# Attention into a gated feed-forward: the first three token chunks take the f-tiles in three groups

## The chip, the cores and the metric

One core of a Trainium2 chip runs the whole program. The metric is the device time of one execution in microseconds. The engines are named as in the profile: PE (TensorE, matmuls), DVE (VectorE), ACT (ScalarE), POOL (GpSimd) and SP (the queue that issues the plain transfers).

## What is computed

Eight batches of eight-head attention (576 positions, head size 64) feed a gated feed-forward over all 8 x 576 = 4608 tokens. Four heads see a window of 32 positions, four see every 32nd position, so most of the score matrix is never formed.

```python
scores = (q @ k.T) / sqrt(64)                     # heads 0-3: 0 <= i-j < 32; heads 4-7: i >= j and i%32 == j%32
attn = exp(scores - max); attn = attn / (attn.sum(-1) + 1e-9)
x = (attn @ v) -> [4608, 512]                     # heads side by side
h = x @ w_in                                      # [4608, 2048]
sp = maximum(h, 0) + log1p(exp(-abs(h)))
out = (h * erf(sp)) @ w_out                       # [4608, 512]
```

## The kernel before

**Tiles.** The tokens form 12 chunks of 384; the 2048 hidden columns form 16 f-tiles of 128. One `ftile` is one chunk by one f-tile, so there are 192, in the order chunk by chunk, f = 0 to 15 inside. A first product (`mm1`, L585, 12 matmuls: `w_in` and x each as a high and a low part, the low-by-low term left out) fills a PSUM bank `h`; a chain of five DVE and six ACT operations makes the gated value and splits it into `ghi` and `glo` (n1 to n7, gate, prod, split_hi, split_lo, L590 to L626); a second product (`mm2`, L656, three matmuls for each of three token tiles t) adds `ghi` and `glo` times `w_out` into the PSUM banks `o0`, `o1`, `o2`. After f-tile 15 of a chunk ACT copies each `o` bank to an SBUF buffer `ob` (L671) and SP stores it. There are three `h` banks, one bank for each of the three `o`, and one buffer `ps` of two banks.

**Weights.** The weights arrive as 64-bit words. Each of the 32 groups of 128 x 512 (16 of `w_in`, 16 of `w_out`) takes four DVE operations and one ACT operation: `bits0` (L536), `bits1` and `bits2` (L543, L549), the ACT copy of the high part (L554), and `split_lo_w` (L557). They pass through a staging buffer of the tag `ob`, of which there are three, shared with the `ob` of the stores. The f-tiles 4s to 4s+3 need the four `w_in` groups of s; f-tile f needs the `w_out` group f.

**Attention.** `heads` handles a pair of heads of one batch, so there are 32 pairs. A pair is: scores on PE (L320, for the first two batches with the mask added by PE, L333), maximum and difference on DVE, exponent on ACT, sum and reciprocal on DVE, normalisation on POOL (`norm`, L418), transposes on PE (L427), a copy on ACT, the product with v on PE (L446), and a split of x into `xhi` and `xlo`. Chunks 0 to 2 need batches 0 and 1 (chunk 0 batch 0 alone), and so on by twos. For batch 0 the scores and the transposes lie in `h` or `o` banks (`B0`), three of its pairs lie in weight buffers not yet filled (`HOME`), and each pair's exponent adds up its row sums on ACT (L392, one operation for each 64 columns). Batch 1 uses the buffer `ps` alone for scores, transposes and output.

**Order.** `Plan` puts all operations on five engine queues when the program is built: each operation has a key (a due time from the tables of constants), and a list schedule with estimated durations takes the one with the lowest key among those that can start soonest. The result is a fixed order for each engine; on the chip an engine waits at whatever instruction is next in its order. Until the first `mm1`, PE's free time is filled with dummy matmuls (`warm`, L751).

Of the kernel before, what the change touches and what calls it, by code (L numbers as in the profile page):

```python
# [8 lines left out]
F32 = mybir.dt.float32  # L9
# [19 lines left out]
PRO = 74.154117  # L29
SLOT = 8.3314687  # L30
MM2 = 14.137159
W1K = (7.7180495, 48.67362, -5.03539, 67.675242)
W1S = (6.27419, 17.806925, 11.8133, 26.168915)
W2K = 61.550152
W2S = 10.390137
A0K = -5.727881
A0S = 1.5429374
A0D = 20.718269
A1K = 99.646963
A1S = -4.8860706  # L40
A1D = -7.3440005
QE = (15.200212, 8.5225749)
QO = (-5.0071746, 2.7270014)
QD = (0.4017474, 1.2188811, 1.98055, 1.78394, 1.3902936)
B0 = (("h", "h"), ("o0", "o1"), ("h", "h"), ("o0", "o1"))
HOME = (None, (7, 8, 9), (10, 11, 12), (13, 14, 15))
ASH = 2.7979051
ADT = 2.5612463
BACKLOG = 1.1130116

# [35 lines left out]

def sub_block(t, j):

    if t == 4:
        return 16 + j % 2  # L90
    return 4 * (t // 2) + j + 8 * (t % 2)
# [10 lines left out]
class Op:  # L102
    def __init__(self, eng, dur, key, emit, after, new, use, earliest):
        self.eng, self.dur, self.key, self.emit, self.earliest = eng, dur, key, emit, earliest
        self.after, self.new = list(after), list(new)
        self.start = self.end = None
        self.locks = eng == "pool" or eng == "dve" and emit.__name__ in TWO
        for b in self.new + list(use):
            b.users.append(self)


class Plan:
# [8 lines left out]
    WINDOW = 70  # L121
# [25 lines left out]
    def order(self):  # L147
# [4 lines left out]
        while left:  # L152
# [24 lines left out]
            if e == "sp":  # L177
                free[e] = t + 0.6
                dma = max(dma, t + 0.6) + o.dur
                o.end = dma + 2.0  # L180
            else:
                o.end = free[e] = t + o.dur
                if o.locks:
                    held[e] = o.end
# [7 lines left out]
def attention_moe(  # L192
# [25 lines left out]
    con = cpool.tile([P, NCON], BF16, name="con")  # L218
    mask_l = con[:, :320]
# [27 lines left out]
    def heads(b, hp, key, dt, ring, before=(), pe_mask=False, pool_norm=True, act_sum=False, banks=None, home=None):  # L247
# [5 lines left out]
        if home is None:  # L253
            qk = [buf("apool", "qk", [P, WQ], f"qk_{pid}")]
            v = [buf("apool", "v", [P, WV], f"v_{pid}")]
        else:
            qk = [buf("wpool", f"w{NFC + f}", [P, 2 * SW], f"qk{f}_{pid}") for f in home[:2]]
            v = [buf("wpool", f"w{NFC + home[2]}", [P, 2 * SW], f"v_{pid}")] + qk[1:]
        sm = buf("apool", "sm", [P, 2, 384], f"sm_{pid}")
        pt = buf("apool", "pt", [P, 2, 384], f"pt_{pid}")  # L260
# [10 lines left out]
        t = s if banks else region(None, "t")  # L271
# [14 lines left out]
        def keys(rows, k0):  # L286
# [24 lines left out]
        def scores():  # L311
# [5 lines left out]
            for t, j, h, m in todo:  # L317
# [5 lines left out]
                    keys(rows, q0),  # L323
# [113 lines left out]
        def av():  # L437
# [5 lines left out]
            for m, a, h in todo:  # L443
# [3 lines left out]
                    px[h * D : (h + 1) * D, m, a * n : (a + 1) * n],  # L447
# [5 lines left out]
        def views(m, x):  # L453
            base = (b % 2) * S
            if loc:
                n = 320 if m else 256
                return px[:, m, :n], x[:, base + 256 * m : base + 256 * m + n]
            nr = 14 if m else 18
            dst = x[:, base : base + S].rearrange("p (a r) -> p a r", r=32)[:, :, 18 * m : 18 * m + nr]
            return px[:, m, : 18 * nr].rearrange("p (r a) -> p a r", a=NA), dst  # L460
# [14 lines left out]
        lq = add("sp", P * 4 * (WL if loc else WS) / 3.6e5, key - 8.0, load_qk, new=qk)  # L475
        lv = add("sp", P * 4 * (VL if loc else VS) / 3.6e5, key - 7.0, load_v, [lq], v[:1], v[1:])
        d_s = 0.85 if loc else 0.95
        if pe_mask:
            d_s += 2 * cols / 2400.0 + 0.05
        o_s = add("pe", d_s, key, scores, [lq, *o_con, *before], [*s, sm], qk)  # L480
        o_n, first = [], []
        for i, p in enumerate(parts):
# [3 lines left out]
            if not pe_mask:  # L486
                o = add("dve", dve(n), key + QD[0] * dt + e, mask(i), [o], [], [z])
            o = add("dve", dve(n), key + QD[0] * dt + 0.05 + e, maxi(i), [o] + first[:1], [mx] if i == 0 else [], [z, mx])
            first.append(o)
            if act_sum:  # L490
                o = add("dve", 0.12, key + QD[0] * dt + 0.1 + e, negate(i), [o], [], [mx])
                o = add("act", 0.33 * n / 64, key + QD[1] * dt + 0.1 + e, exp_sum(i), [o] + first[1:2], [rc] if i == 0 else [], [z, mx, sm, rc])
            else:
                o = add("dve", dve(n), key + QD[0] * dt + 0.1 + e, less(i), [o], [], [z, mx, sm])
                o = add("act", act(n), key + QD[1] * dt + 0.1 + e, exp(i), [o], [], [sm])
                o = add("dve", dve(n), key + QD[2] * dt + e, total(i), [o] + first[1:2], [rc] if i == 0 else [], [sm, rc])
            first.append(o)
            o = add("dve", 0.25, key + QD[2] * dt + 0.05 + e, invert(i), [o], [], [rc])
            if pool_norm:
                o = add("pool", 0.1 + n / 450.0, key + QD[2] * dt + 0.1 + e, norm(i), [o], [], [sm, rc])  # L500
            else:
                o = add("dve", dve(n), key + QD[2] * dt + 0.1 + e, norm(i), [o], [], [sm, rc])
            y = t[i] if len(t) > 1 else t[0]
            o = add("pe", 0.33 * (p.stop - p.start), key + QD[3] * dt + e, turn(i), [o] + first[2:3], ([pt] if i == 0 else []) + ([y] if not banks else []), [sm, y])
            first.append(o)
            o = add("act", act(384 * (p.stop - p.start), 0.06), key + QD[3] * dt + 0.1 + e, fetch(i), [o], [], [y, pt])
            o_n.append(o)
        o_v = add("pe", 1.3 if loc else 0.95, key + QD[4] * dt, av, o_n + [lv] + ring, [px], [pt, *v])
        done = []
        for m in range(2):  # L510
            n = (320 if m else 256) if loc else (252 if m else 324)
            hi, lo = split(m)
            o = add("act", act(n, 0.06), key + QD[4] * dt + 0.1 + 0.01 * m, hi, [o_v], [], [px])
            done.append(add("dve", dve(n), key + QD[4] * dt + 0.2 + 0.01 * m, lo, [o], [], [px]))
        return done, o_v


    def weight(i, src, rows, sl, key):
# [41 lines left out]
        if wide:  # L560
            op = add("sp", P * 8 * n / 3.6e5, key - 8.0, load, new=[words])
            op = add("dve", dve(n, 0.5), key, bits0, [op], [w], [words])
            op = add("dve", dve(n), key + 0.1, bits1, [op], [], [w, words])
            op = add("dve", dve(n), key + 0.2, bits2, [op], [], [w, words])
        else:
            op = add("sp", P * 4 * n / 3.6e5, key - 8.0, load, new=[w])
        op = add("act", act(n), key + 0.3, split_hi, [op], [pair], [w])
# [3 lines left out]
    def ftile(k, ready):  # L571

        c, f = k // NFC, k % NFC
# [57 lines left out]
        def at(offset):  # L631
            return v0 + (offset + 0.3) * SLOT / 3.9

        first = add("pe", 2.09, v0, mm1, ready[0] + mm1_first[-1:], [ph])
        o = add("act", tp, at(0.0), n1, [first], [a], [ph])
        o = add("dve", td, at(0.6), n2, [o], [], [ph, a])
        o = add("act", ta, at(1.2), n3, [o], [], [a])
        o = add("act", ta, at(2.25), n4, [o], [bb], [a])
        o = add("dve", td, at(2.9), n5, [o], [], [a, ph])
        o = add("dve", td, at(3.5), n6, [o], [], [a, bb])  # L640
        o = add("act", ta, at(4.35), n7, [o], [], [bb])
        o = add("act", ta, at(5.55), gate, [o], [], [bb])
        o = add("dve", td, at(6.2), prod, [o], [], [bb, ph])
        o_h = add("act", tp, at(6.8), split_hi, [o] + hi_of[-1:], [ghi], [ph])
        hi_of.append(o_h)
        o_l = add("dve", td, at(7.9), split_lo, [o_h], [glo], [ph, ghi])
        last = []
        for t in range(NTT):
            if f == 0:
                o_ps[t] = buf("ps_o", f"o{t}", [P, DM], f"o{t}_{c}")  # L650
# [197 lines left out]
```

## Time and profile before

| | |
|---|---|
| median of 3 runs (lowest to highest) | 960.15 us (959.93 to 961.97) |
| the profiled execution's own time | 961.45 us |
| its span, first to last instruction | 959.7 us |
| busy: PE, DVE, ACT, POOL | 933.7, 689.4, 652.0, 47.5 us |
| mean granted TensorE clock | 0.987 |
| DMA packets | 64.23 MB, of which 9.44 MB written |

The numbers of busy time are sums over the whole span. PE counts the dummy matmuls as busy, so a busy PE in the first tenth says little. The first 120 us differ from the rest in what they wait for, and are read by windows.

### The profile page before, as it was taken

Reading aid. Unit: us, or ns where it says so; the run is one execution under the profiler, and the core shown is the slowest. Engines: PE = TensorE matmul, PEld = TensorE weight load, DVE = VectorE, ACT = ScalarE, POOL = GpSimd, SP = SyncE. Lnnn points to the kernel's source line nnn. Section 1 sums busy time; section 2 is a strip of 40 time slices with the busy share of each in tenths; the row PEclk is TensorE's granted clock in tenths of the full one; section 3 lists DMA queues with packets and bytes.
Section 4 is the critical chain, followed back from the end, with each engine's and each line's share of the span. In section 5 each row is a group of like instructions: output and inputs, shape, how many; then the busy total and the mean of one; then the engine's idle time right before and its main releaser. Section 6 shows DMA issues by size and latency. Waiting matters only on the chain.

```text
span 959.7 us, 20411 instructions
## 1 busy us (share of the span) xinstructions
PE 933.7 (97%) x8380; PEld 832.5 (87%) x8380; DVE 689.4 (72%) x1350; ACT 652.0 (68%) x1437; POOL 47.5 (5%) x40
## 2 busy tenths in 40 slices
PE   8948999999999999999999999999999999999998
PEld 6837788998888899988888889988888899999997
DVE  4999999766776666676878566666777666666664
ACT  5555778676667766766667766766667766666765
POOL 1111000000101000000001000000000000000000
PEclk9978999999999999999999999999999999999999
DMA  9963101003111210002312210001220200000000
GB/s 354 395 245 129 54 1 60 28 26 109 67 53 62 66 48 1 34 27 62 112 54 70 79 32 22 34 27 45 101 81 2 95 1 1 34 1 1 34 1 33
DMA packets 19822, 64.23 MB, mean 67 GB/s; under 512 B 2192, under 2 KB 2320, under 8 KB 19728
## 3 DMA queue, kind: packets, MB, share of 16 engines
q1 hardware_dynamic: 19728, 62.92, 18.5%
q8 instruction: 66, 1.08, 0.4%
q14 instruction: 28, 0.23, 0.1%
HBM read 53.48 MB, written 9.44 MB: 66 GB/s over the span
## 4 chain that ended last, share of the span: by engine, by line
PE 89%; DVE 8%; issue 1%; ACT 1%; DMA 1%; SPq 0%
PE o L656 41%; PE h L585 40%; PE x L446 3%; PE s L320 2%; PE t L427 2%; DVE w L543 2%; DVE w L549 1%; DVE pair L557 1%; DMA words<-w_in 1%; DVE w L536 1%; DVE a L590 1%; ACT sm L392 1%; DVE mx L356 0%; DVE xlo L470 0%; DVE b L590 0%
## 5 line engine op out<-in xcount | busy, mean ns | idle before, releaser
L656 PE MATMUL o<-pair,ghi 128*128 128x512 f32 x1152 | 365.4, 398 | 0.0
L585 PE MATMUL h<-xhi,pair 128*128 128x384 f32 x1536 | 303.3, 339 | 1.9 <-DVE glo L626 1.8
L585 PEld LDWEIGHTS h<-xhi,pair 128*128 128x128 f32 x1536 | 273.9, 189 | 13.4 <-DVE glo L626 3.1
L656 PEld LDWEIGHTS o<-pair,ghi 128*128 128x128 f32 x1152 | 210.8, 189 | 39.0
L593 ACT ACTIVATE b<-b 128x384 f32<-128x384 f32 x384 | 201.3, 524 | 58.4 <-DVE b L590 55.0
L656 PE MATMUL o<-pair,glo 128*128 128x512 f32 x576 | 226.8, 394 | 0.0
L590 DVE SCALAR_TENSOR_TENSOR a<-a,h 128x384 f32<-128x384 f32 x192 | 105.7, 550 | 87.1 <-ACT b L593 87.1
L585 PE MATMUL h<-xlo,pair 128*128 128x384 f32 x768 | 165.1, 336 | 0.0
L593 ACT ACTIVATE a<-a 128x384 f32<-128x384 f32 x192 | 100.8, 525 | 80.9 <-DVE a L590 80.9
L620 DVE TENSOR_TENSOR h<-b,h 128x384 f32<-128x384 f32 x192 | 107.1, 558 | 50.1 <-ACT b L593 50.1
L593 ACT ACTIVATE a<-h 128x384 f32<-128x384 f32 x192 | 93.1, 485 | 72.9 <-PE h L585 71.6
L626 DVE TENSOR_TENSOR glo<-h,ghi 128x384 fp32r<-128x384 f32 x192 | 106.2, 553 | 49.1 <-ACT ghi L623 48.2
L585 PEld LDWEIGHTS h<-xlo,pair 128*128 128x128 f32 x768 | 136.9, 189 | 0.0
L590 DVE SCALAR_TENSOR_TENSOR a<-h,a 128x384 f32<-128x384 f32 x192 | 106.4, 554 | 41.8 <-ACT a L593 41.6
L656 PEld LDWEIGHTS o<-pair,glo 128*128 128x128 f32 x576 | 108.4, 188 | 23.6
L623 ACT CAST ghi<-h 128x384 fp32r<-128x384 f32 x192 | 91.1, 474 | 39.0 <-PE o L656 29.5
L590 DVE SCALAR_TENSOR_TENSOR b<-b,a 128x384 f32<-128x384 f32 x192 | 110.9, 578 | 2.0
L593 ACT ACTIVATE b<-a 128x384 f32<-128x384 f32 x192 | 100.1, 522 | 3.2
L418 POOL TENSOR_TENSOR sm<-sm,r 128x768 f32<-128x768 f32 (+3 forms) x36 | 47.3, 1314 | 699.1 <-DVE r L411 546.1
L446 PEld LDWEIGHTS x<-pt,v 64*64 64x64 f32 x1848 | 32.9, 136 | 11.5 <-issue 3.6
L320 PEld LDWEIGHTS s<-qk 64*32 64x32 f32 (+1 forms) x1872 | 25.1, 121 | 17.2 <-issue 13.3
L446 PE MATMUL x<-pt,v 64*64 64x32 f32 (+1 forms) x1848 | 36.8, 223 | 1.9 <-ACT pt L433 1.8
(40 smaller groups left out, 508.1 us busy)
## 6 DMA issues: line engine op xcount, KB each, us to landing
v<-v_loc SPq DMA_DIRECT2D x15, 640.0 KB, 4.0
out<-ob SPq DMA_DIRECT2D x36, 256.0 KB, 2.2
qk<-qk_loc SPq DMA_DIRECT2D x15, 592.0 KB, 4.0
qk<-qk_str SPq DMA_DIRECT2D x14, 608.0 KB, 3.9
words<-w_in SPq DMA_DIRECT2D x16, 512.0 KB, 9.8
words<-w_out SPq DMA_DIRECT2D x16, 512.0 KB, 9.2
v<-v_str SPq DMA_DIRECT2D x16, 384.0 KB, 3.1
qk<-qk_str SPq DMA_DIRECT2D x4, 304.0 KB, 8.0
```

The costliest lines, as they stand in the source:

```text
L320: yield nc.tensor.matmul(bank(s, h)[m * j : m * (j + 1), 64 * t : 64 * (t + 1)], queries(rows, q0, m), keys(rows, q0), start=(h, j) not in ...
L418: yield (nc.gpsimd if pool_norm else nc.vector).tensor_tensor(out=d, in0=d, in1=spread(rc, i), op=ALU.mult)
L427: yield nc.tensor.transpose(bank(t, h)[:, 128 * w : 128 * w + 128], sm[:, h, c : c + 128], ident)
L446: yield nc.tensor.matmul(px[h * D : (h + 1) * D, m, a * n : (a + 1) * n], values(rows, (2 * a + h) * D), pt[rows, h, c : c + n], start=Tru ...
L543: yield nc.vector.scalar_tensor_tensor(out=wb, in0=words[:, :, 1], scalar=0xC0000000, in1=wb, op0=ALU.bitwise_and, op1=ALU.bitwise_or)
L585: yield nc.tensor.matmul(ph[:, :CH], win[4 * s + cc][:, w, fs], x[cc][:, c0 : c0 + CH], start=(i == 0), stop=(i == len(terms) - 1))
L590: yield nc.vector.scalar_tensor_tensor(out=out, in0=in0, scalar=scalar, in1=in1, op0=op0, op1=op1)
L593: yield nc.scalar.activation(dst, src, func, bias=bias[i], scale=scale)
L620: yield nc.vector.tensor_tensor(out=ph[:, :CH], in0=bb.tile, in1=ph[:, :CH], op=ALU.mult)
L623: yield nc.scalar.copy(ghi.tile, ph[:, :CH])
L626: yield nc.vector.tensor_tensor(out=glo.tile, in0=ph[:, :CH], in1=ghi.tile.bitcast(F32), op=ALU.subtract)
L656: yield nc.tensor.matmul(po.tile, g[:, ts], wout[f][:, w], start=(f == 0 and i == 0), stop=(f == NFC - 1 and i == 2),)
```

## The change

**The order of the f-tiles.** For chunks 0 to 2 the f-tiles are taken in three groups, 0 to 3, 4 to 7 and 8 to 15: all three chunks go through a group before the next group begins (`SEGS`). The 9 segments each end with the three `o` banks being copied to `ob`. The first segment of a chunk stores its partial sum as before; the two later ones add theirs to the output in memory by a transfer that POOL issues (`accumulate`), each waiting for the landing of the earlier transfer to the same rows. That makes 18 accumulating transfers of 256 KB and 18 more ACT copies. Chunks 3 to 11 go as before.

**The pairs ahead of them.** All eight pairs of batches 0 and 1 now use one set of banks for scores, transposes and output (`own=True`), among `h`, `o` and `ps` (`PAIRS`). Seven lie in weight buffers, three of them with a fourth buffer for the exponents; the transposed values overwrite the queries (`View`). The normalisation of pair 0_0 goes to DVE. The row sums on ACT are used by 0_0, 0_1, 0_3, 1_1 and 1_3. Loads of the weight groups that share a buffer with a pair are ordered behind it (`w_load`).

**The rest.** An exponent of one column is put ahead so that ACT loads its table early (`first_exp`). All keys are new tables (`FT` for the steps of an f-tile, `KW` for weights, `KP` for pairs), `WINDOW` is 250.

```diff
-PRO = 74.154117
-SLOT = 8.3314687
+PRO = 28
+SLOT = 4.5
+FT = (2.47591, 2.44924, 3.30228, ...
+PAIRS = (
+    (("h", "h"), None, True, False),
+    (("o0", "o1"), (4, 5, 6), True, True),
+    (None, (7, 20, 21, 22), False, True),
+    (("h", "h"), (23, 8, 9, 10), True, True),
+    (("o0", "o1"), (11, 24, 25, 26), False, True),
+    (None, (27, 12, 13), True, True),
+    (("o0", "o1"), (14, 15, 28), False, True),
+    (None, (29, 30, 31), True, True),
+)
+SEGS = ((0, 0, 4), (1, 0, 4), (2, 0, 4), (0, 4, 8), (1, 4, 8), (2, 4, 8), (0, 8, 16), (1, 8, 16), (2, 8, 16))
...
-        px = buf("ps_a", "ps", [P, 2, 512], f"x_{pid}")
...
-        t = s if banks else region(None, "t")
+        t = s if own else region(None, "t")
+        px = s if own else region(None, "x")
...
-            if f == NFC - 1:
+            if f == last_f:
...
+                def accumulate(t=t, ob=ob):
+                    yield nc.gpsimd.dma_start(
+                        out=out[c * CH + t * P : c * CH + (t + 1) * P, :], in_=ob.tile, accum_op=ALU.add
+                    )
...
-                add("sp", P * DM * 4 / 3.6e5, o.key + 0.1, store, [o], [], [ob])
+                if first_f == 0:
+                    stored[c, t] = add("sp", P * DM * 4 / 3.6e5, o.key + 0.1, store, [o], [], [ob])
+                else:
+                    o = add("pool", 1.2, o.key + 0.1, accumulate, [o, stored[c, t]], [], [ob])
+                    o.tail = 2.5
+                    stored[c, t] = o
...
-        for c in range(3 * p2, 3 * p2 + 3):
-            chunk(c)
+        for c, f0, f1 in SEGS if p2 == 0 else [(c, 0, NFC) for c in range(3 * p2, 3 * p2 + 3)]:
+            chunk(c, f0, f1)
```

**Where it shows in the order: DVE among the early f-tiles.** This is DVE's order before, between the gated value of f-tile 4 and `glo` of f-tile 5. In the names, `w` is the staging buffer of a weight group with its number, `pair` its finished form, and `a`, `b`, `h`, `glo` are the buffers of f-tiles.

```order
L536 TENSOR_SCALAR w_22_1592<-words_918 128x512
L590 SCALAR_TENSOR_TENSOR b_1581<-b_1581,a_1491 128x384
L557 TENSOR_TENSOR pair_1587<-w_14_1449,pair_1587 128x512
L543 SCALAR_TENSOR_TENSOR w_22_1592<-words_918,w_22_1592 128x512
L626 TENSOR_TENSOR glo_1607<-h_1392,ghi_1584 128x384
L549 SCALAR_TENSOR_TENSOR w_22_1592<-words_918,w_22_1592 128x512
L590 SCALAR_TENSOR_TENSOR a_1594<-h_1562,a_1594 128x384
L620 TENSOR_TENSOR h_1429<-b_1581,h_1429 128x384
L557 TENSOR_TENSOR pair_1624<-w_22_1592,pair_1624 128x512
L536 TENSOR_SCALAR w_23_1633<-words_954 128x512
L626 TENSOR_TENSOR glo_1638<-h_1429,ghi_1629 128x384
```

And this is DVE's order after the change, between the f-tiles 6 and 8 (counted in the new order).

```order
L589 TENSOR_SCALAR w_20_1526<-words_967 128x512
L644 SCALAR_TENSOR_TENSOR a_1510<-h_1477,a_1510 128x384
L596 SCALAR_TENSOR_TENSOR w_20_1526<-words_967,w_20_1526 128x512
L674 TENSOR_TENSOR h_1369<-b_1492,h_1369 128x384
L602 SCALAR_TENSOR_TENSOR w_20_1526<-words_967,w_20_1526 128x512
L644 SCALAR_TENSOR_TENSOR a_1510<-a_1510,h_1477 128x384
L644 SCALAR_TENSOR_TENSOR a_1541<-h_1512,a_1541 128x384
L644 SCALAR_TENSOR_TENSOR b_1534<-b_1534,a_1510 128x384
L610 TENSOR_TENSOR pair_1548<-w_20_1526,pair_1548 128x512
L680 TENSOR_TENSOR glo_1563<-h_1369,ghi_1555 128x384
```

Before, six of eleven rows are of weight groups; after, four of ten, because twelve f-tiles share the first eight groups.

**POOL's queue.** Before, POOL holds the normalisations of the pairs and nothing else; these are the last of the first two batches and the first of the next.

```order
L418 TENSOR_TENSOR sm_2_1004<-sm_2_1004,r_2_1068 128x768
L418 TENSOR_TENSOR sm_1_1114<-sm_1_1114,r_1_1214 128x2x320
L418 TENSOR_TENSOR sm_0_1264<-sm_0_1264,r_0_1345 128x2x320
L418 TENSOR_TENSOR sm_0_1517<-sm_0_1517,r_0_2204 128x2x320
L418 TENSOR_TENSOR sm_1_2160<-sm_1_2160,r_1_2306 128x2x320
```

After, the accumulating transfers (`out<-ob`) stand among them; the number behind `ob` is the f-tile whose segment it closes.

```order
L468 TENSOR_TENSOR sm_3_1082<-sm_3_1082,r_3_1165 128x768
L731 DMA out<-ob_15_2019 128x512
L731 DMA out<-ob_15_2028 128x512
L468 TENSOR_TENSOR sm_0_1425<-sm_0_1425,r_0_2046 128x2x320
L731 DMA out<-ob_15_2098 128x512
L731 DMA out<-ob_19_2212 128x512
L731 DMA out<-ob_19_2271 128x512
L731 DMA out<-ob_19_2274 128x512
L731 DMA out<-ob_23_2390 128x512
```

The first normalisation of batch 2 now stands behind two transfers, and 16 further transfers follow up to the end of the third chunk's last segment.

More of the change, by code (lines that the diff above doesn't have):

```diff
@@ L120 @@
     PATIENCE = 0.002
-    WINDOW = 70
+    WINDOW = 250
     def __init__(self, bufs):
@@ L181, in order @@
             else:
-                o.end = free[e] = t + o.dur
+                free[e] = t + o.dur
+                o.end = free[e] + o.tail
                 if o.locks:
-                    held[e] = o.end
+                    held[e] = free[e]
             for b in o.new:
@@ L244, in act, with heads @@
         return fixed + n / 1200.0
-    def heads(b, hp, key, dt, ring, before=(), pe_mask=False, pool_norm=True, act_sum=False, banks=None, home=None):
+    def heads(b, hp, keys, ring, before=(), pe_mask=False, pool_norm=True, act_sum=False, banks=None, home=None, own=False):
         loc = hp < 2
@@ L284, in queries, with keys_of @@
             return qk[0][rows, q0 : q0 + n]
-        def keys(rows, k0):
+        def keys_of(rows, k0):
             k0 += wq if home is None else 0
@@ L322, in scores @@
                     queries(rows, q0, m),
-                    keys(rows, q0),
+                    keys_of(rows, q0),
                     start=(h, j) not in used,
@@ L474, in heads @@
         add = plan.add
-        lq = add("sp", P * 4 * (WL if loc else WS) / 3.6e5, key - 8.0, load_qk, new=qk)
-        lv = add("sp", P * 4 * (VL if loc else VS) / 3.6e5, key - 7.0, load_v, [lq], v[:1], v[1:])
-        d_s = 0.85 if loc else 0.95
+        slab = pt if home is None else qk[0]
+        k_q, k_v, k_s, k_m, k_n, k_t, k_x = keys
+        lq = add("sp", P * 4 * (WL if loc else WS) / 3.6e5, k_q, load_qk, new=qk)
+        lv = add("sp", P * 4 * (VL if loc else VS) / 3.6e5, k_v, load_v, [lq], v[:1], v[1:])
+        d_s = 0.95 if loc else 1.0
         if pe_mask:
             d_s += 2 * cols / 2400.0 + 0.05
-        o_s = add("pe", d_s, key, scores, [lq, *o_con, *before], [*s, sm], qk)
+        o_s = add("pe", d_s, k_s, scores, [lq, *o_con, *before], [*s, sm], qk)
         o_n, first = [], []
@@ L503, in heads @@
             y = t[i] if len(t) > 1 else t[0]
-            o = add("pe", 0.33 * (p.stop - p.start), key + QD[3] * dt + e, turn(i), [o] + first[2:3], ([pt] if i == 0 else []) + ([y] if not banks else []), [sm, y])
+            o = add("pe", 0.33 * (p.stop - p.start) + 0.05, k_t + e, turn(i), [o] + first[2:3], ([pt] if i == 0 and home is None else []) + ([y] if not own else []), [sm, y])
             first.append(o)
-            o = add("act", act(384 * (p.stop - p.start), 0.06), key + QD[3] * dt + 0.1 + e, fetch(i), [o], [], [y, pt])
+            o = add("act", act(384 * (p.stop - p.start), 0.06), k_t + (0.1 + e), fetch(i), [o], [], [y, slab])
@@ L507, in heads @@
             o_n.append(o)
-        o_v = add("pe", 1.3 if loc else 0.95, key + QD[4] * dt, av, o_n + [lv] + ring, [px], [pt, *v])
+        o_v = add("pe", 1.35 if loc else 1.0, k_x, av, o_n + [lv] + ring, [] if own else px, [slab, *v] + (px if own else []))
         done = []
@@ L701, in attention_moe @@
             rows, sl = slice(c * P, (c + 1) * P), slice(f, f + SW)
-            op, pair = weight(i, w_in, rows, sl, W1K[i // 4] + W1S[i // 4] * (i % 4))
+            op, pair = weight(i, w_in, rows, sl, KW[i // 8][i % 8])
             w1.append(op)
@@ L706, in attention_moe, with chunk @@
         rows, sl = slice(f * P, (f + 1) * P), slice(0, DM)
-        op, pair = weight(NFC + f, w_out, rows, sl, W2K + W2S * f)
+        op, pair = weight(NFC + f, w_out, rows, sl, KW[2 + f // 8][f % 8])
         w2.append(op)
         wout.append(pair)
-    def chunk(c):
+    def chunk(c, f0, f1):
         need = [o for b in (2 * (c // 3), 2 * (c // 3) + 1) for o in x_of.get((b, c % 3), [])]
-        for f in range(NFC):
-            k = c * NFC + f
+        for f in range(f0, f1):
             ready = (need + w1[4 * (f // 4) : 4 * (f // 4) + 4], [w2[f]])
-            mm1_of[k], _ = ftile(k, ready)
-            mm1_first.append(mm1_of[k])
+            o, _ = ftile(len(mm1_first), c, f, f0, f1 - 1, ready)
+            mm1_first.append(o)
+            mm1_of[c] = o
     def chunks_of(b, hp, m):
```

173 lines of the change are left out of this document (104 added, 69 removed), and 4 rows, old and new, of the table KW.

## The prediction

> **What bounds the kernel now.** I read the page first, then windows, then PE's timeline and the chain of waits over the first 150 us.
>
> ```profile
> PE 933.7 (97%) x8380; PEld 832.5 (87%) x8380; DVE 689.4 (72%) x1350; ACT 652.0 (68%) x1437; POOL 47.5 (5%) x40
> DVE  4999999766776666676878566666777666666664
> PEclk9978999999999999999999999999999999999999
> ```
>
> Over the span PE is the bound and DVE is not. Slices 2 to 7 of DVE's row (each 24 us) say otherwise for the first stage, and PE's clock falls below full there alone. The windows have it in numbers; columns are length, then busy time and instructions of PE, PEld, DVE, ACT, POOL, granted clock, DMA share and GB/s.
>
> ```profile
> 0.00:24.00 24.00, 19.96 (x396) 16.26 (x397) 12.00 (x34) 13.21 (x70) 4.68 (x9) 1.00 0.94 354
> 24.00:48.00 24.00, 23.93 (x378) 21.17 (x377) 23.89 (x53) 13.59 (x47) 3.31 (x3) 1.00 1.00 395
> 48.00:72.00 24.00, 11.52 (x255) 9.60 (x254) 23.31 (x41) 12.83 (x25) 3.72 (x2) 0.71 0.66 245
> 72.00:96.00 24.00, 20.13 (x343) 17.84 (x342) 22.49 (x44) 12.90 (x27) 2.99 (x2) 0.87 0.39 129
> 96.00:120.00 24.00, 22.12 (x183) 19.09 (x182) 24.00 (x50) 16.91 (x38) 0.00 (x0) 0.99 0.17 54
> 120.00:144.00 24.00, 24.00 (x115) 21.46 (x114) 22.78 (x46) 17.59 (x37) 0.00 (x0) 0.94 0.00 1
> ```
>
> From 24 to 120 us DVE is busy 93.7 of 96 us. The transfers run at full share until 48 us and then fall off, so they feed DVE and don't bound it later. PE's timeline shows the two ends of that stage (start, length, what, idle before it).
>
> ```profile
> 45.14 1.66 PE L585 MATMUL h<-xhi,pair 128*128 128x384 f32 x8
> 55.61 0.93 PE L320 MATMUL s<-qk 64*64 64x64 f32 x48 [2.65 <-DVE sm L368]
> 118.32 2.11 PE L585 MATMUL h<-xhi,pair 128*128 128x384 f32 x8 [1.83 <-DVE glo L626]
> ```
>
> The first product of f-tile 0 starts at 45.14. The last wait of PE on DVE ends at 118.32, where f-tile 10 starts. Counted in the timeline between the two, PE begins ten first products and does 21 of the three-matmul groups of the second (seven f-tiles). From 118.32 to the end at 959.7 PE never waits: 841.4 us for 182 first products, 555 groups and 24 pairs. The chain shows PE's pace there, and DVE's pace ahead of it, where each instruction starts as the last one lets it (start, length, what).
>
> ```profile
> 24.69 0.34 DVE w L536
> ...
> 49.23 0.60 DVE pair L557
> 50.44 0.60 DVE w L543
> 51.04 0.47 DVE a L590
> ...
> 52.71 0.87 DVE mx L356
> ...
> 124.32 2.10 PE h L585 x12
> 126.42 2.08 PE o L656 x9
> ```
>
> So a first product takes 2.10 and a second 2.08, 0.69 for each group. On DVE a weight group takes 0.34 + 3 x 0.60 = 2.14 us and an f-tile 5 x 0.47 = 2.35. Before, an f-tile of chunk 0 needs a `w_out` group and, on average, a `w_in` group of its own: 2.35 + 4.28 = 6.6 us of DVE against 4.18 of PE. That is why PE idles.
>
> **The three groups.** The first 12 f-tiles after the change need 8 weight groups, and so do the next 12: (8 x 2.14 + 12 x 2.35) / 12 = 3.8 us of DVE an f-tile against 4.18 of PE. The next 24 need 16 and cost the same. DVE then lies just under PE, where it was half as much again above it. What is left is attention of batches 0 and 1 on DVE, which must come first in part.
>
> I count both orders alike: DVE's work up to a certain `glo`, then PE's work left.
>
> Before, from the `bits0` at 24.7 (the first row of that fence) to the `glo` of f-tile 7 (ending at about 118.2) DVE's order holds 22 `bits0`, 45 `bits1` and `bits2`, 23 `split_lo_w` (48.2 us by the paces above), 43 operations of f-tiles (20.1) and 46 of attention (18.0, at 0.87 for 768 columns and in proportion): 86.3 us. It took 93.5, a factor of 1.085. The lost 8% are stretched or waiting instructions, such as the one below.
>
> After, I take as mark the second product of the 17th f-tile (k = 16), near which the sum stays level from k = 1 to k = 32. From the first `w_out` group (row 66 of DVE's order) to that `glo`, DVE's order holds 18 + 35 + 17 operations of weights (37.2 us), 89 of f-tiles (41.7) and 29 of attention (10.5): 89.3 us. At the mark PE has done 20 first products and 48 groups against 10 and 21 at 118.32, so what is left is 841.4 - 10 x 2.10 - 27 x 0.69 = 801.7 us, the end's stores included.
>
> The factor lies between 1.00 (DVE busy 24.00 of 24 in the window from 96) and 1.085. I take 1.06: most of the stretch has few pairs, as after 96 us, but it begins with three. That makes 94.7.
>
> **The start.** The page gives the sizes of the transfers, and the chain and DVE's timeline the first steps of attention.
>
> ```profile
> v<-v_loc SPq DMA_DIRECT2D x15, 640.0 KB, 4.0
> qk<-qk_loc SPq DMA_DIRECT2D x15, 592.0 KB, 4.0
> qk<-qk_str SPq DMA_DIRECT2D x14, 608.0 KB, 3.9
> v<-v_str SPq DMA_DIRECT2D x16, 384.0 KB, 3.1
> ```
>
> ```profile
> 7.46 0.49 DVE L356 TENSOR_REDUCE mx<-s 128x5 f32<-128x320 f32 x1 [3.35 <-PE s L333]
> ```
>
> ```profile
> 13.39 3.09 ACT sm L392 x20
> ```
>
> Up to and with the first `w_out` group, the new order of SP loads 256 KB of constants, 4800 KB of queries and keys, 3712 KB of values (eight pairs' queries and seven pairs' values) and five weight groups of 512 KB, 11.6 MB. By the windows 8.5 MB come in 24 us (354 GB/s) and the other 3.1 in 7.9 at 395 GB/s: 31.9, and about 2 to land. DVE has 22.7 us of work ahead of that row and can't begin the maxima before about 7.5 us (the row above), so 30.2 without a wait. I take 35 for row 66, with 33 to 39 as bounds. The lower is the transfer alone; the upper adds 4, a third of the 12 us that DVE is idle before 24 us in the present order.
>
> PE's first product needs a normalisation, transposes, a copy and a product with v behind that, 3 us, so it starts at about 38 instead of 45.14.
>
> **The sum.** 35 + 94.7 + 0.2 (the semaphore to PE) + 801.7 = 931.6 us of span. The profiled execution took 961.45 for its span of 959.7, 1.75 more, so 933.3 on its scale. The median of the runs lies 1.3 under it: **932 us**, 2.9% less than 960.15.
>
> **Costs put at nothing.** The 18 more copies of `o` to `ob` and 18 accumulating transfers have these nearest rows.
>
> ```profile
> L671 ACT COPY ob<-o 128x512 f32<-128x512 f32 x36 | 20.7, 584 | 8.1 <-PE o L656 7.0 <-DMA out<-ob 0.2
> out<-ob SPq DMA_DIRECT2D x36, 256.0 KB, 2.2
> words<-w_in SPq DMA_DIRECT2D x16, 512.0 KB, 9.8
> ```
>
> The copies are 18 x 0.58 = 10.5 us of ACT spread over some 190 us, where ACT has 24 - 17.6 = 6.4 us free in each 24. If that cover were gone, up to 10.5 would be added. PE meets a segment's end with 3.5 us or more of other work between the last use of a bank and the next, against 0.58 plus ACT's queue. No row shows an accumulating transfer. Between 2.2 (a store) and 9.8 us (a load in a full queue) I take 4, nearer the store, since after 48 us the queues are mostly empty. The `ob` buffers are also the staging buffers of weights, and by DVE's order about 16 instructions, 8 us, lie between a copy and the `bits0` that takes its buffer, so 4 are hidden and 9.8 are not quite. A shorter wait for the table load on ACT and the dropped dummy matmuls give nothing beyond the start already counted. Chunks 3 to 11 have in the new order the same distance from first to second product, 8.5 us of PE work at least and 16 on average, so PE stays as it was there.
>
> [...] One row of DVE stands out, beside one of its kind and the POOL instruction at the same time (two timelines).
>
> ```profile
> 66.57 2.03 POOL L418 TENSOR_TENSOR sm<-sm,r 128x768 f32<-128x768 f32 x1 [6.25 <-ACT pair L554]
> ```
>
> ```profile
> 65.51 0.54 DVE L590 SCALAR_TENSOR_TENSOR a<-a,h 128x384 f32<-128x384 f32 x1
> ...
> 67.19 1.83 DVE L590 SCALAR_TENSOR_TENSOR b<-b,a 128x384 f32<-128x384 f32 x1
> ```
>
> A DVE operation of that size takes 0.54 otherwise, so a POOL instruction cost DVE 1.3 us. If each accumulating transfer costs DVE as much, the nine that stand ahead of the 32nd f-tile add 9 x 1.3 = 11.7 us to the sum. I leave it out, because a transfer issue isn't a POOL instruction that reads rows of 768, and count it as a rival. [...]
>
> **The rivals.**
> - *PE alone bounds from the first product.* If DVE keeps up, PE starts at 38 and does 20 x 2.10 + 48 x 0.69 + about 8 of pairs = 83 us to the mark, 121 in all: 121 + 801.7 = 922.7 of span, 923 as median. For it: 3.8 us of DVE against 4.18. Against it: the three pairs still open and the factor of 1.085 seen.
> - *The start doesn't move.* The change then does only half of what it says. Pairs 0_1 and 0_0 share ACT's one-by-one exponents, 20 of them (6.2 us by the row of 3.09 for ten and their ten read-outs), and DVE again waits half of the first 24 us. With the first product at 45 again, the sum is about 8 more: 940.
> - *POOL's transfers stretch DVE:* 943 to 944, as above. Against it: only 18 such events.
> - *The staging buffers are held, and it gets slower.* In DVE's order three runs of weight groups (13, 14 and 26; 15 and 25; 27, 28 and 31) take buffers that an `ob` of an accumulating transfer has just had. DVE stops there, with every f-tile's chain queued behind it. With a landing time L each run costs L - 8. At 9.8 us that is 5 (937); it takes three runs of 9.4, so L above 17 us, to lose the whole 28. Against it: the slowest median landing in the page is 9.8.
>
> **Chances.** 0.63 for the forecast (925 to 938); 0.14 for PE alone; 0.10 for a start that doesn't move; 0.09 for POOL's port; 0.04 for held buffers beyond 17 us. About 0.2% (2 us) is what a measurement of this kernel can tell from no change, by the spread of its three runs. All but the last case end below 958, and next to nothing lies within 2 us of 960: faster 0.95, same 0.01, slower 0.04. The range of 921 to 945 runs from PE alone with a transfer-bound start to POOL's port with a full 1.3 us.
>
> **What would show it.** Right: the first `h` row of PE at 36 to 40 us; DVE busy over 23 of 24 us in the windows from 36 to 130 and PE waiting there in short pieces, most of them for `glo`; granted clock back at 1.00 earlier than 120; nothing but the usual after 200 us. Wrong: PE full from 40 on (PE alone); a first `h` row near 45; DVE's two-input rows of 1.5 us and more next to the issues of `out<-ob` on POOL; a `bits0` row with an idle time of several us before it that a DMA of `out` ended.

## The result, and the profile after

The changed kernel takes 938.54 us (median of 4 runs, 938.04 to 938.87) against 961.06 us for the kernel before on the same chip: a ratio of 0.976, 95% interval 0.974 to 0.978. The forecast was 932 with a range of 921 to 945; the measured time lies half a microsecond above the 925 to 938 that had a chance of 0.63. The profiled execution took 938.84 us for a span of 937.1, so the sum's 931.6 of span was 5.5 short.

From the page, the busy rows and the two rows of tenths that were shown of before:

```profile
PE 917.3 (98%) x8298; PEld 818.1 (87%) x8298; DVE 684.1 (73%) x1357; ACT 658.6 (70%) x1478; POOL 59.7 (6%) x57
...
DVE  4799998998757767676876577766687866566664
...
PEclk9999999999999999999999999999999999999999
```

DVE's full stretch ends sooner, and PE's clock no longer falls below 0.9 in any slice. The windows in the same columns as before:

```profile
24.00:48.00 24.00, 20.45 (x423) 16.97 (x420) 19.06 (x47) 13.63 (x62) 3.12 (x4) 0.93 0.99 382
48.00:72.00 24.00, 21.99 (x416) 18.59 (x413) 22.91 (x52) 19.51 (x61) 4.59 (x4) 1.00 0.83 301
72.00:96.00 24.00, 23.61 (x196) 20.93 (x194) 23.81 (x49) 18.50 (x42) 0.00 (x0) 1.00 0.51 187
96.00:120.00 24.00, 23.21 (x116) 20.38 (x115) 23.98 (x49) 19.76 (x43) 0.00 (x0) 1.00 0.09 33
120.00:144.00 24.00, 23.84 (x125) 21.59 (x124) 22.88 (x47) 20.55 (x44) 3.66 (x4) 1.00 0.24 56
```

From 48 to 120 us PE is busy 68.8 us of 72 where it was 53.8 before, and DVE is as full as it was. Before 48 us, though, DVE is busy only 19.06 of 24 where it was 23.89: the start got worse. PE's timeline shows where (start, length, what, idle before it):

```profile
15.28 0.34 PE L370 MATMUL s<-qk,qk 64*64 64x64 f32 x7 [0.70 <-issue]
...
28.56 0.54 PE L370 MATMUL s<-qk,qk 64*32 64x64 f32 x35 [3.20 <-issue]
...
49.71 1.66 PE L639 MATMUL h<-xhi,pair 128*128 128x384 f32 x8
```

The first product starts at 49.71 us, later than the 45.14 of before. In the middle of the scores of pair 1_0, PE stops for 3.20 us with "issue" as cause, so nothing that the profile shows held it. The granted clock follows: it is 0.50 from 29.7 to 33.1 us. DVE's timeline pays for the stop:

```profile
9.18 0.89 DVE L406 TENSOR_REDUCE mx<-s 128x5 f32<-128x320 f32 x2 [2.07 <-PE s L383]
...
21.79 1.69 DVE L589 TENSOR_SCALAR w<-words 128x512 uint32<-128x512 uint32 x1
...
31.25 0.56 DVE L406 TENSOR_REDUCE mx<-s 128x6 f32<-128x384 f32 x1 [3.92 <-PE s L383]
...
43.52 0.39 DVE L589 TENSOR_SCALAR w<-words 128x512 uint32<-128x512 uint32 x1
```

DVE waits 3.92 us for scores (those of pair 0_3, queued on PE behind pair 1_0's), and row 66, the first `w_out` group, comes at 43.52. From the first product on, the waits of PE up to 160 us are few; these are the two largest (what waits, on what, us in total, times, longest):

```profile
PE h L639 <- DVE glo L680: 1.3, 5, 0.4
PE o L710 <- DVE xlo L520: 1.1, 1, 1.1
```

Summed from the timeline, PE is idle 4.8 us from the first product to the end; before it was 18.1. The page also shows the new transfers:

```profile
out<-ob SPq DMA_DIRECT2D x36, 256.0 KB, 2.1
...
out<-ob POOLq DMA_DIRECT2D x18, 256.0 KB, 5.1
```

An accumulating transfer lands 5.1 us after its issue, a store 2.1.

### The profile page after: what moved, and what is told of

It is laid out like the page before. It is cut to its first block, busy times and chain, and to the rows that moved or that the text cites. A ratio compares the mean times of both kernels' runs of the same rounds, so it can differ in the third digit from the quotient of the medians.

```text
span 937.1 us, 20346 instructions
## 1 busy us (share of the span) xinstructions
PE 917.3 (98%) x8298; PEld 818.1 (87%) x8298; DVE 684.1 (73%) x1357; ACT 658.6 (70%) x1478; POOL 59.7 (6%) x57
## 3 DMA queue, kind: packets, MB, share of 16 engines
q8 instruction: 65, 1.06, 0.5%
## 4 chain that ended last, share of the span: by engine, by line
PE 80%; DVE 10%; issue 5%; ACT 3%; DMA 2%; POOL 1%; SPq 0%; POOLq 0%; ACTq 0%
PE h L639 35%; PE o L710 35%; PE s L370 3%; PE x L496 3%; DVE a L644 2%; PE warm L819 2%; PE t L477 2%; DVE glo L680 1%; DVE b L644 1%; DVE w L596 1%; DMA out<-ob 1%; DVE w L602 1%; DVE h L674 1%; ACT b L647 1%; DVE pair L610 1%
## 5 line engine op out<-in xcount | busy, mean ns | idle before, releaser
L710 PE MATMUL o<-pair,ghi 128*128 128x512 f32 x1152 | 360.9, 395 | 1.3 <-DVE xlo L520 1.1
L639 PEld LDWEIGHTS h<-xhi,pair 128*128 128x128 f32 x1536 | 268.4, 188 | 15.2 <-DVE glo L680 6.8
L644 DVE SCALAR_TENSOR_TENSOR b<-b,a 128x384 f32<-128x384 f32 x192 | 106.5, 555 | 1.8
L468 POOL TENSOR_TENSOR sm<-sm,r 128x768 f32<-128x768 f32 (+3 forms) x35 | 44.3, 1267 | 518.4 <-DVE r L461 286.8
L406 DVE TENSOR_REDUCE mx<-s 128x12 f32<-128x768 f32 (+3 forms) x37 | 28.9, 786 | 8.9 <-PE s L383 8.6
L725 ACT COPY ob<-o 128x512 f32<-128x512 f32 x54 | 30.4, 586 | 4.0 <-PE o L710 2.6
L496 PEld LDWEIGHTS x<-pt,v 64*64 64x64 f32 x1392 | 24.5, 135 | 7.8 <-issue 3.8
```

Source lines behind the costliest of these rows:

```text
L406: yield nc.vector.tensor_reduce(out=mx[:, parts[i], :units], in_=wide(of(s, i)), axis=mybir.AxisListType.X, op=ALU.max)
L468: yield (nc.gpsimd if pool_norm else nc.vector).tensor_tensor(out=d, in0=d, in1=spread(rc, i), op=ALU.mult)
L496: yield nc.tensor.matmul(bank(px, m)[h * D : (h + 1) * D, a * n : (a + 1) * n], values(rows, (2 * a + h) * D), pt[rows, h, c : c + n], sta ...
L639: yield nc.tensor.matmul(ph[:, :CH], win[4 * s + cc][:, w, fs], x[cc][:, c0 : c0 + CH], start=(i == 0), stop=(i == len(terms) - 1))
L644: yield nc.vector.scalar_tensor_tensor(out=out, in0=in0, scalar=scalar, in1=in1, op0=op0, op1=op1)
L710: yield nc.tensor.matmul(po.tile, g[:, ts], wout[f][:, w], start=(f == first_f and i == 0), stop=(f == last_f and i == 2),)
```

## The experiments

Ratios are to the kernel before on the same chip, with 95% intervals; the changed kernel's own is 0.9762 (0.9741 to 0.9783). Where two intervals overlap I compare the profiles of the two kernels, f-tile by f-tile.

| kernel | median, us | ratio (interval) | first product, us |
|---|---|---|---|
| the changed kernel | 938.54 | 0.9762 (0.9741 to 0.9783) | 49.71 |
| groups_undone | 959.33 | 0.9985 (0.9974 to 0.9995) | 44.11 |
| two_groups | 942.08 | 0.9797 (0.9775 to 0.9818) | 45.20 |
| plain_stores | 936.80 | 0.9745 (0.9728 to 0.9762) | 48.86 |
| ob_four | 936.89 | 0.9749 (0.9723 to 0.9774) | 49.55 |
| constants_first | 939.49 | 0.9774 (0.9756 to 0.9792) | 48.79 |
| constants_first_ob_four | 937.46 | 0.9758 (0.9735 to 0.9781) | 49.71 |
| dve_less | 935.91 | 0.9742 (0.9721 to 0.9763) | 49.56 |
| pe_less | 939.63 | 0.9779 (0.9759 to 0.9799) | 48.96 |
| both_less | 934.61 | 0.9727 (0.9705 to 0.9750) | 48.37 |
| no_dummies | 940.88 | 0.9794 (0.9775 to 0.9814) | 52.09 |
| wide_dummies | 942.17 | 0.9808 (0.9785 to 0.9831) | 51.80 |
| narrow_dummies | 945.06 | 0.9838 (0.9812 to 0.9863) | 53.41 |

### Which part carries the gain

```diff
-SEGS = ((0, 0, 4), (1, 0, 4), (2, 0, 4), (0, 4, 8), (1, 4, 8), (2, 4, 8), (0, 8, 16), (1, 8, 16), (2, 8, 16))
+SEGS = ((0, 0, 16), (1, 0, 16), (2, 0, 16))                                               # groups_undone
+SEGS = ((0, 0, 8), (1, 0, 8), (2, 0, 8), (0, 8, 16), (1, 8, 16), (2, 8, 16))              # two_groups
...
```

Both runs also have the due times `KW` and `KP` fitted anew to their order; those lines are left out here.

> The pairs ahead and the banks stay, but chunks 0 to 2 each take all 16 f-tiles in one go (no accumulating transfer, 9 stores); the due times of the weight groups and of the first 16 pairs are fitted to the new order. If the grouping carries the gain: up to the second product of the 17th f-tile DVE has to finish 31 or 32 weight groups where it now finishes 18, 13 x 2.14 x 1.046 = 29 us more, less what PE can draw forward of later pairs (up to 10): 957 to 967 us, PE waiting again in long pieces for glo. If the pairs ahead carry it: no more than 945.

> The f-tiles in two groups, 0 to 7 and 8 to 15, with 9 accumulating transfers instead of 18; due times refitted. If DVE's work per f-tile decides as the prediction counts it: the first 8 f-tiles need all of 8 + 8 weight groups, some 6 more by the 9th f-tile than with groups of four, 6 x 2.14 = 13 us, and at the 24th f-tile the count is the same as now, so 945 to 951. If PE alone is the bound and DVE has room, or if the accumulating transfers cost something: 936 to 940.

Without the groups nearly all of the gain is gone: 959.33 us, 0.15% under the kernel before. The pairs ahead and the banks are still in it, and its first product even starts at 44.11. Its windows:

```profile
48.00:72.00 24.00, 17.22 (x337) 14.21 (x336) 23.36 (x51) 19.26 (x67) 4.59 (x4) 0.93 0.82 300
72.00:96.00 24.00, 16.16 (x173) 13.25 (x174) 23.57 (x47) 9.54 (x18) 0.00 (x0) 0.76 0.64 226
96.00:120.00 24.00, 20.91 (x98) 19.57 (x97) 22.80 (x46) 18.32 (x38) 0.00 (x0) 0.88 0.00 0
120.00:144.00 24.00, 22.16 (x110) 19.32 (x109) 24.00 (x49) 17.51 (x37) 0.00 (x0) 1.00 0.00 1
```

DVE is as full as in the changed kernel, and PE is busy a quarter less from 48 to 96 us, at a lower clock. The second product of the 17th f-tile stands at 161.4 instead of 139.3. Of the waits of PE from 44 to 160 us, some 20 us in all, these are the two largest:

```profile
PE s L370 <- DMA qk<-qk_loc: 5.6, 1, 5.6
PE h L639 <- DVE glo L680: 5.4, 4, 3.1
```

So the long pieces of waiting for `glo` that were expected are only a part; in the longest one PE stands before scores whose queries have not landed. It is DVE that shows what sets the pace: from 48 to 160 us it waits for only 2.5 us in all, and up to the `glo` of the 17th f-tile its order holds all 32 weight groups, where the changed kernel has finished 21. So the grouping works as predicted, by spreading DVE's weight work over more f-tiles. What the groups would bring without the pairs ahead was not run.

With two groups the time is 942.08, between the two expectations (936 to 940 and 945 to 951). Its first product starts 4.5 us earlier, and the second product of the tenth f-tile (k = 9) stands 3.8 us later than in the changed kernel: 8.3 us lost in between, where 13 were expected.

### Whether DVE or PE bounds the stretch

```diff
# dve_less: bits2 only for the first groups
+            if i in (0, 1, 2, 3, 16, 17):
                 yield nc.vector.scalar_tensor_tensor(out=wb, in0=words[:, :, 0], scalar=29, ...)
# pe_less: shorter first products
+            terms = terms[:8] if k < 24 else terms
# both_less: both edits
```

> The bits2 operation (0.60 us of DVE) is left out for 26 of the 32 weight groups, all but those of the first four w_in and first two w_out, so their lowest three bits are missing; the rest and all orders stay. Up to the second product of the 17th f-tile that is some 16 operations, 9.6 us. If DVE alone sets the pace there, as in the prediction: 9 to 10 us less, 928 to 930. If PE alone does (it is idle 4.84 us in all after the first product): at most 4, 934.5 to 938. If both are level, between: 933 to 936.

> The first products of the first 24 f-tiles do 8 of their 12 matmuls (the low part of x is left out): 24 x 4 x 0.176 = 16.9 us less of PE; orders stay. If PE alone sets the pace from the first product on: 14 to 17 us less, 922 to 925. If DVE alone sets it up to the 17th f-tile: only the f-tiles behind the mark count (4 to 8 of them, 0.7 each), 3 to 6 less, 933 to 936. If both are level: between, 926 to 932, with PE waiting for glo in most f-tiles.

> Both cuts at once: bits2 left out for 26 weight groups, and 8 of 12 matmuls in the first products of the first 24 f-tiles. Alone the first brought 2.6 us and the second nothing. If DVE and PE are level in that stretch and nothing else is near, the two together bring nearly all of DVE's 9.6 us: 927 to 931. If ACT, or a buffer, stands just behind them: 933 to 936, no more than the DVE cut alone. If the DVE cut was hidden by something other than PE: 935 to 936.

Taking 16.9 us off PE brings nothing (939.63). The waits of PE up to 160 us in that kernel:

```profile
PE h L640 <- DVE glo L681: 10.1, 17, 1.5
```

So DVE sets the pace, as the sum had it: in the profile, PE's saving turned into waits for `glo`. All three expected ranges are missed even so, that for DVE alone (933 to 936) too: the profile leads by 1.8 us up to the 40th f-tile, 0.75 of it from an earlier first product, and then loses 2.6. Taking 9.6 us off DVE brings 2.6 (935.91, which fits both the range for PE alone and the one for both level; pe_less speaks against PE alone): PE's waits for `glo` go from 1.3 to 0.6, and PE is then the bound.

Both together bring 3.9 as median. By their profiles both_less leads by 6.9 us up to the 40th f-tile (1.3 of it from an earlier first product) and loses 2.7 of that between the 40th and the 43rd, as pe_less loses 2.6 there. That loss has a cause of its own, shown in the last section. Up to that point the lead beyond the start is 5.6 us, against 3.2 with the DVE cut alone, so the expected 7 to 11 fail. The trace shows what stands in the way. These are, from 48 to 200 us, first the busy times in the columns of above, then the waits of PE and DVE:

```profile
48.00:200.00 152.00, 140.28 (x1056) 118.29 (x1052) 138.91 (x282) 125.04 (x291) 13.49 (x15) 1.00 0.37 107
```

```profile
PE h L641 <- DVE glo L682: 7.5, 12, 1.2
DVE a L646 <- ACT b L649: 4.2, 9, 1.6
DVE h L676 <- ACT b L649: 3.6, 5, 1.6
```

None of the three engines is full any more. PE waits for `glo`, and DVE waits 7.8 us for results of ACT in the chain from `h` to `glo`, where in the changed kernel it is 3.9. So that chain, which goes back and forth between the two engines, has taken over. Whether ACT's own work (82% busy) or the order of the chain's steps is the limit was not tested.

### What the accumulating transfers cost

```diff
# plain_stores
-                    yield nc.gpsimd.dma_start(out=out[...], in_=ob.tile, accum_op=ALU.add)
+                    yield nc.sync.dma_start(out[...], ob.tile)
# ob_four: the pool's buffers only, the orders stay
+            n = 4 if tag == "ob" else bufs[tag]
-            return pools[pool].tile(shape, dtype, tag=tag, name=name, bufs=bufs[tag])
+            return pools[pool].tile(shape, dtype, tag=tag, name=name, bufs=n)
```

> The 18 accumulating transfers from POOL become plain stores from SP to the same rows, so the partial sums are not added up; all other instructions and orders stay. If they cost nothing, as the prediction has it: the same as now, 938.5 within 1. If POOL's port stretches DVE by 1.3 us for each of the nine ahead of the 32nd f-tile, or held staging buffers stop DVE: 927 to 935.

> The staging buffers of the tag ob are four instead of three; every order stays. In the profile DVE waited 0.68 us at 177.7 and ACT 0.17 at 105.7 for a transfer of out to free one, and in the runs that started 0.9 us earlier ACT waited 0.74 to 1.01 there and the lead was gone by the 12th f-tile. If held buffers cost that: the two waits vanish, 0.5 to 1 us less, 937.5 to 938. If they are hidden: 938.5 within 0.5.

Plain stores take 936.80, between the two expectations. They end 2.3 us earlier in the profile, 0.85 of it from an earlier start. But of that start 0.2 is left by the 14th f-tile, before the first accumulating transfer (136.9 us), so the transfers cost 1.5 to 2.1 us. DVE isn't stretched by them: of its 29 instructions beside an issue on POOL, none is over 0.012 us longer than the median of its kind. The changed kernel's DVE timeline has two places, and PE's timeline the echo of the second:

```profile
143.23 0.43 DVE L589 TENSOR_SCALAR w<-words 128x512 uint32<-128x512 uint32 x1 [0.96 <-DMA out<-ob]
...
177.69 0.43 DVE L589 TENSOR_SCALAR w<-words 128x512 uint32<-128x512 uint32 x1 [0.68 <-DMA out<-ob]
```

```profile
181.37 1.67 PE L639 MATMUL h<-xhi,pair 128*128 128x384 f32 x8 [0.62 <-DVE glo L680]
...
186.04 1.68 PE L639 MATMUL h<-xhi,pair 128*128 128x384 f32 x8 [0.26 <-DVE glo L680]
```

A `bits0` waits 0.96 us, and another 0.68 us, for an accumulating transfer to free its buffer (an ACT copy at 158.93 waits 0.89 for one too); after the second PE waits 0.62 and 0.26 for `glo`. With a fourth buffer DVE's and PE's waits here are gone, ACT's is 0.17, and the profile leads by 1.9 us from the 28th f-tile on, of which 1.06 come between the 25th and the 28th. That is more than the 0.5 to 1 us expected. This is the version with the shortest time that leaves no work out: 936.89, ahead of both kernels in the median; its interval overlaps the changed kernel's.

### Why the start is late

```diff
# constants_first
-    for op in plan.order():
+    for op in sorted(plan.order(), key=lambda op: op.emit is not load_consts):
```

> The load of the constants is put first in SP's order, ahead of the queries of pair 0_1; nothing else moves. It landed at 6.5 us as third, and the first scores waited for it until 7.35 (5.64 before the change). If PE is full from the first product on, so that the start counts one to one: the first scores at about 5.7, and 1 to 1.7 us less, 937 or a little under. If the start is set by something later (a stall of PE at 25 us, the transfers): 938.5 within 0.5, and the first product at 49.7 as now.

> Constants first and four staging buffers. Constants first alone moved the first product from 49.7 to 48.8 and left 0.4 us of it at the end of its profile. If the staging buffer ate the rest: 1.3 to 1.8 us less than now, 936.7 to 937.2. If DVE's pace eats it: 937.7 to 938.5.

Neither time falls in an expected range (939.49 and 937.46). The constants land at 3.4 us instead of 6.5, but the first scores start at 6.5 and 7.2 in these two kernels: they now wait for the queries, which are the same bytes further back. Unchanged orders had their first scores anywhere from 6.1 to 7.8, so nothing is gained. Of the 0.9 us by which constants_first did begin earlier, part went at 105 us, at ACT's copy:

```profile
105.19 0.59 ACT L725 COPY ob<-o 128x512 f32<-128x512 f32 x1 [0.74 <-DMA out<-ob]
```

The other suspect is the stop of PE. It would fit if PE's program came in blocks and PE stopped where the next block had not come; the texts below call this the fetching theory. I counted PE's weight loads and matmuls: the stops named "issue" before the first product come after 445, 953 and 1462 of them. Three kernels change nothing but the dummy matmuls, and so shift the program against that count.

```diff
# no_dummies
-    plan.filler = (first, warm, warm_ps, mm1_first[0])
# wide_dummies: every second one, with 512 columns
+        if next(dummies) % 2 == 0:
+            yield nc.tensor.matmul(warm_ps[:, :512], ident_b, con[:, :512], start=True, stop=True)
# narrow_dummies: each as two of 128
+        for n in (0, 128):
+            yield nc.tensor.matmul(warm_ps[:, n : n + 128], ident_b, con[:, n : n + 128], start=True, stop=True)
```

> All dummy matmuls but the first are left out (153 of them, each a weight load and a matmul); every other instruction and order stays. PE stopped for 3.20 us at 25.4 us with nothing but 'issue' as cause, after 953 of its weight loads and matmuls, for 0.70 after 445 and 0.35 after 1462. If the stall belongs to a place in PE's instruction stream (fetching of instructions), it stays near those counts: without the 61 dummies (122 instructions) ahead of it, the 953rd comes after the scores of pair 1_0, those scores run through at 25, DVE's idle time of 3.9 us at 27 to 31 shrinks to 1 or less, and the first product comes 1 to 3 us earlier, at 47 to 49 instead of 49.7; the time then 936 to 938. If it is a wait for data or a semaphore, it stays in the scores of pair 1_0 at 25.4 to 28.6, and the time at 938.5 within 1. If the dummies are needed for the clock, the granted clock in the first 48 us falls below 0.9 and the time is 938 to 941.

> Every second dummy matmul is left out and the others have 512 columns instead of 256, so that PE is as busy as now with 77 fewer dummies (154 fewer instructions). Fetching theory: the 953rd instruction comes about 60 instructions later in the program, near the end of pair 1_0's scores or just behind them, so the stall moves by that much and the time hardly, 937 to 938.5. Data theory: the stall stays at the same matmul (35 matmuls of those scores still to come). Clock: as now, 0.93 to 1.00 in the first 48 us.

> Each dummy matmul of 256 columns is two of 128, so PE is as busy as now with twice the dummies (308 instructions more up to the first product). Fetching theory: PE still stops only after 445, 698, 953, 1208, 1462 weight loads and matmuls within 10, and each stop ends 1.2 to 1.6 us after a packet of 16 KB on the instruction queue has landed; these counts now come earlier in the program, the 953rd ahead of the scores of pair 1_0, and there is one more before the first product, so the first product at 49 to 53 and the time 938 to 942. Any other theory of the stall (data, a semaphore, the mask): it stays in the scores of pair 1_0, with 3.2 us, and the time at 938.5.

PE's stops of over a microsecond for "issue" in no_dummies:

```profile
25.66 1.07 PE L496 MATMUL s<-pt,v 64*64 64x32 f32 x22 [2.78 <-issue]
...
32.23 0.92 PE L370 MATMUL s<-qk,qk 64*64 64x64 f32 x25 [2.67 <-issue]
...
41.26 1.40 PE L370 MATMUL s<-qk,qk 64*32 64x64 f32 x80 [1.09 <-issue]
```

And in narrow_dummies:

```profile
14.04 0.58 PE L370 MATMUL s<-qk,qk 64*64 64x64 f32 x24 [0.92 <-issue]
...
26.54 0.64 PE L496 MATMUL s<-pt,v 64*64 64x32 f32 x7 [3.41 <-issue]
...
32.83 0.80 PE L370 MATMUL s<-qk,qk 64*64 64x64 f32 x18 [1.65 <-issue]
```

The instructions that stop are others each time, but the counts are 698 and 953 for the first two of no_dummies, 445, 954 and 1209 in narrow_dummies, and 444, 696, 950 and 1455 for those of half a microsecond and more in wide_dummies. Every one lies within 10 of 445 + 255 n. (The third of no_dummies, after 1112, does not; what it is stays open. Nor does every later stop with this label: groups_undone has one of 3.79 us after 2135, with no packet under way. So the label alone does not tell.) On the queue named "instruction" the trace has 65 packets of 16,384 bytes in the changed kernel, and PE's 2 x 8298 loads and matmuls make 65.1 times 255; with no_dummies it is 64 packets and 63.9. In the profile of the changed kernel such a packet arrives from 26.13 to 27.25, and PE goes on at 28.56; in no_dummies from 23.13 to 24.23 and from 29.68 to 30.79, and PE goes on at 25.66 and 32.23. From a packet's end to PE's next instruction it is 1.3 to 1.6 us at the three stops of the changed kernel and 1.4 at these two of no_dummies.

So PE stops where a new block of its own instructions has not come. By the counts a block is 255 loads and matmuls, and it comes as one packet of 16,384 bytes. The packet that PE needs at 953 starts at 26.13, and PE has entered the block before it, at 698, at 22.6. A block is dear in the start because its packet starts late. PE enters a new block at 9.4, 15.3, 22.6, 28.6, 34.9 and 41.2 us, and the next packet starts 3.3 to 4.2 us later, at a DMA share of 0.94 in the first 24 us and 0.99 in the next; by the same count it is 1.4 at most from 103 us on, where the mean share is 0.16. With the packet's own 1.1 and the 1.3 to 1.6 behind it, a block costs 6 to 7 us in the start (two_groups once got one in 3.0): of the five blocks between these six times PE passed none in less than 5.8 us. That the loads in the queues delay the packets is the likely cause, but not shown: in the kernel before, with shares of 0.94 and 1.00, the same count gives 0.9 to 3.2 us for the first six packets, and PE has no such stop ahead of its first product. Scores and products with v are very short matmuls (35 scores take 0.54 us at 28.56, eight matmuls of a first product 1.66 at 49.71), so they run into it.

The fetching theory holds for the place of the stops, but its times were expected wrongly, those of narrow_dummies (945.06) and wide_dummies (942.17) and the first products above all: all three variants start theirs 2 to 4 us later, at 51.8 to 53.4. With fewer dummies the stop after 698 falls on a product with v at 23 us, where it did not stop PE before. Narrow dummies need one block more. The clock may be a second cause, which these runs don't separate from the stops: from 24 to 48 us the granted clock is 0.50 with no dummies (940.88 fits the expectation for the clock), 0.86 with wide and 0.72 with narrow ones, against 0.93. None of the three is a remedy. Whether less loading at 20 to 45 us would shorten the stops was not tried.

## Why the prediction came near, and which of its steps failed

The parts of the sum, as predicted and as measured in the profile after:

| part | predicted, us | measured, us |
|---|---|---|
| row 66 of DVE | 35 | 43.5 |
| from row 66 to `glo` of the 17th f-tile | 94.7 | 93.4 |
| to its second product | 0.2 | 2.4 |
| PE's rest | 801.7 | 797.8 |
| span | 931.6 | 937.1 |

The total is near in part by luck: two terms were 8.5 and 2.2 us too short, two others 1.3 and 3.9 too long.

- *The start* is the term that was mis-sized, by 8.5 us, and outside its bounds of 33 to 39. The step "DVE has 22.7 us of work ahead of that row", first maxima at 7.5, and some 5 us of waits became: first maxima at 9.18, 8.1 us of waits (3.92 of them behind PE's stop) and 26.3 of work and stretched rows, such as the `bits0` of 1.69 us at 21.79 where one takes 0.42. The bound from the transfers was right (the words of that group land at 35.2; the 2 us to land were an estimate, next to the 2.2 of a store) but not the one that ended last. I took the start for a matter of transfers and DVE, and looked at PE only behind them.
- *The first product at about 38 instead of 45.14* failed with it. It came at 49.7. The gain that I had put down to an earlier start was not there at all; the rival "the start doesn't move", with 8 us more at row 66, had it right at 43. Its 940 is missed only by the handover to PE (2.2 more) and PE's rest (3.9 less). But its reason was another: of DVE's waits up to row 66 only 1.3 us are for ACT's exponents, and the first product came 4.6 later than its 45.
- *DVE's stretch* was right: 93.4 us for 89.3 of work, a factor of 1.046 where I took 1.06. (The order before holds 44 `bits1` and `bits2` and not 45, so its factor was 1.09.) pe_less and dve_less show that DVE sets it, with PE some 3 us behind.
- *PE alone bounds* was the rival with the best sight of PE: idle for only 4.8 us after the first product. But PE's work could be cut by 16.9 us without gain, so it is level with DVE, not alone. The 2.4 us at the mark are this: PE was busy with other work when `glo` was ready. The 0.2 for the semaphore was an estimate that no run shows: before, PE's product at 118.32 starts 0.05 us behind the end of the `glo` it waits for (117.70, 0.57 long).
- *PE's rest* is 3.9 us shorter. From the mark on, a matmul of the second product takes 0.2330 us against 0.2358 in the stretch of before that the term came from, 4.4 us over 1583 of them. PE changes between the two products and attention 313 times from the mark on, and before 328 times over the same products; that this is the cause was not tested.
- *The accumulating transfers* landed in 5.1 us, where I took 4 between 2.2 and 9.8. They weren't free: 1.5 to 2.1 us, mostly through held buffers, so that rival was right in kind and far off in size. "By DVE's order about 16 instructions, 8 us, lie between a copy and the `bits0`" left out that POOL issues one transfer after another (three take 2.64 us from 171.34). The rival of 943 to 944, "POOL's port" in the recorded texts, cost nothing on DVE (0.012 us at most on one of the 29 instructions beside an issue). A port is shown by no run, only the 1.83 us of the one row beside a normalisation.
- *Of the signs,* DVE above 23 of 24 us came true from 60 to 130 us (22.94 from 36 to 60), clock 1.00 from 48 us on, PE's waits for `glo` in short pieces (five, at most 0.41).

## What to carry to other kernels

If an engine that prepares data limits the first stage, reorder the loops so that each prepared piece is used more often before the next is needed; here twelve f-tiles instead of four shared eight weight groups, and 18 accumulating transfers cost 1.5 to 2.1 us for some 20 gained. When two engines are level, cutting either brings little, so try both cuts before trusting one. Count the instructions of short-matmul stretches as well as their time: here, at a DMA share of 0.99, PE's own program came late enough to stop it for 3.20 us, and the stop landed on whatever stood there.

## What the runs showed of the hardware that I had not expected

PE's program is loaded in blocks of 16,384 bytes while it runs, 65 of them in the changed kernel. PE stopped 3.20 us for one there, at a DMA share of 0.99, and 3.41 in narrow_dummies (above).

After a wait of 1.53 us, as much again was lost in clock. In pe_less PE waits at 254.6 us ahead of a pair's product with v, and the next first product takes 3.75 us (257.47 to 261.22); in the changed kernel the same wait is 0.49, and the product takes 2.20 (258.22 to 260.42). (The profile names a DVE operation as the cause; in both_less, at the same place, it names the transfer of the values, 1.67 us.) From pe_less:

```profile
256.18 1.37 PE L496 MATMUL x<-pt,v 64*64 64x32 f32 x72 [1.53 <-DVE b L645]
257.47 2.77 PE L640 MATMUL h<-xhi,pair 128*128 128x384 f32 x8
```

And from the changed kernel:

```profile
256.93 1.37 PE L496 MATMUL x<-pt,v 64*64 64x32 f32 x72 [0.49 <-DVE glo L680]
258.22 1.67 PE L639 MATMUL h<-xhi,pair 128*128 128x384 f32 x8
```

The granted clock from 256 to 262 us is 0.72 in pe_less and 1.00 in the changed kernel, where the same 72 short matmuls stand behind the wait of 0.49; in both_less, with its 1.67, it is 0.76 from 250 to 256.
